# A norm factor kept in PSUM, and a weight split's ramp in PSUM, in a replanned attention and MoE kernel

## The chip, the cores and the metric

The kernel runs on one core of a Trainium2 chip. The metric is the device time of one execution in microseconds; the time of a kernel is the median of its runs.

## The reference

Three steps follow one another, all in float32. Clustered attention on 2 batch elements, 8 heads, 768 positions and a head dimension of 64; its output, 1536 tokens of 512 numbers, goes through a normed gated block and then through a second block.

```python
q_assign = np.argmax(einsum(q_n, c_n)); k_assign = np.argmax(einsum(k_n, c_n))    # 16 clusters per head
scores = np.where(q_assign == k_assign, scale * q @ k.T, -1e9)
attn = softmax(scores);  x = attn @ v                      # per head; heads side by side give x: 1536 x 512
rms = np.sqrt(np.mean(x * x, axis=-1, keepdims=True) + 1e-06)
xn = x / rms * rms_g
g = xn @ w_gate;  h = g * (1.0 / (1.0 + np.exp(-g))) * (xn @ w_val)     # 512 -> 1536
x = h @ w_out                                                            # 1536 -> 512
r = np.maximum(x @ w_in, 0.0);  out = (s * (r * r) + b) @ w_out2         # 512 -> 2048 -> 512
```

## The kernel before

Heads are numbered 0 to 15: 0 to 7 are batch element 0, 8 to 15 batch element 1. For each head the kernel finds the clusters (`assign_*`), the maximum of each row of scores (`rowmax` on TensorE, `rowmax_out` at L424 on VectorE), the scores and their exponentials (L447, L448, L453), splits the exponentials into a half-precision high part (`cast`, on GpSimd at L458 or on ScalarE at L460) and a rest (`rest`, GpSimd, L464), multiplies with the values (L477, L487) and divides (`pv_out`, L498 to L500). The table `pc` in `P` names, per head, the chunks whose cast GpSimd does.

When the eight heads of a batch element are done, `rms_scale` works out one factor per token: it adds the partial sums of squares (L530), scales (L531), and calls `rsqrt` (L506 to L511), which is a shift, a subtraction from a constant and three Newton steps of three operations each, all on VectorE and on tiles of 128x6 in SBUF, named rx, rr and rw. `rms_norm` (L539) multiplies the tokens by it; transposes (L546), `rms_x` (L553, L555) make the operands xh and xl of the next block.

The weights come as 64-bit words that `split_w` turns into float32 and then into a high and a low part. ScalarE makes two ramps of the exponent byte, `a` (L606) and `b` (L607); VectorE joins them to the exponent (L610, from b and a, both in SBUF, into a) and puts the mantissa in (L611, from raw and a, both in SBUF, into a); ScalarE copies the high part (L614), GpSimd subtracts (L617). `wtmp` holds one pair a, b, so that splits follow one another. `plan_weights` plans the splits of four slices of the hidden dimension, f = 0 to 3, three matrices each (j = 0, 1, 2: gate, value, out).

The first two pairs of slices are filler for TensorE inside the attention of heads 8 to 15: `m_mm` (L623), `m_tanh` (L925), `m_gate` (L929), `m_val` (L933), `m_hi` (L937), `m_lo` (L941), `m_pr` (L656). They write PSUM tiles of the tag "g", of which there are two (`b_g=2`). The banks of these two are the second buffer of the row maxima of heads 0 to 7; `switch` closes that pool and opens "g", once the row maxima of head 7 are done (`gsw`).

All of the attention and of this filler is an order written out by a planner (`Plan`): every step is added with its engine, a cost in us, what it reads and writes, the buffers that it takes and a priority; the planner starts the step that can begin first, and among those that can begin within `look` of it the one of least priority value. The leads in `P` (`lt`, `lh`, ... `lr`, `lg`, `lk`, `rg`) set the priorities. Each engine then works through its steps in the planned order, and a step waits only for its inputs and its buffers. What follows the planned part (`run_items`: the other pairs of the first block, and the second block) has a fixed order.

Of the kernel before, what the change touches and what calls it, by code (L numbers as in the profile page):

```python
# [20 lines left out]
F32 = mybir.dt.float32  # L21
# [9 lines left out]
BIG = 2.0 ** 100  # L31

P = dict(
    nat=(1, 1, 1, 1, 1, 1, 1, 1, 1, 1, 1, 1, 1, 1, 1, 1), pc=((0, 1, 2, 3, 4), (3,), (0, 4), (0, 4), (0, 1, 3, 4),
    (4,), (1, 2, 3, 4), (1,), (1, 3, 4), (0, 4), (0, 1, 3), (0,), (0, 1, 2, 3), (2, 3, 4), (0, 1, 2, 3), (0, 1)),
    b_wp=2, b_raw=2, b_hp=4, b_tp=2, b_wt=1, b_q4=3, b_a32=5, b_a16=6, b_vsp=2, b_up=2, pvb=2, b_pm=1, b_g=2,
    b_pv=1, b_s=3, look=(0.2, 0.14, 0.14, 0.0, 1.07), fifo=2.5, ni=1, nx=5, lg=462.36, rg=-6.19, lk=147.75, nd=2,
    l1=53.02, l2=-28.36, li=347.3, ho=(0.0, 0.0, 0.0, 0.0, 0.0, 0.0, 0.0, 0.0, 0.0, 0.0, 0.0, 0.0, 0.0, 0.0, 0.0,
    0.0), lt=(-36.0, -253.71), lh=(-125.63, 332.03), ld=(93.0, -61.97), la=(-0.63, 344.08), le=(563.62, -285.56),
    lm=(118.57, 144.43), lo=(307.47, -175.69), ll=(-131.36, -42.83), lx=(24.87, 357.66), ls=(-128.3, 6.07),  # L40
    lc=(-68.33, 7.5), lv=(-27.58, -184.46), lw=(-142.18, -496.74), ly=(64.26, 270.33), lq=(35.78, -22.17),
    lp=(-408.39, -161.62), lz=(-203.89, -3.37), lr=(11.8, -52.43)
)

class Plan:
# [100 lines left out]
def attention_moe_moe2_kernel(  # L146
# [357 lines left out]
    def rsqrt(y, x, w):  # L504

        nc.vector.tensor_scalar(w.bitcast(I32), x.bitcast(I32), 1, None, op0=ALU.logical_shift_right)  # L506
        nc.vector.tensor_scalar(y.bitcast(I32), w.bitcast(I32), -1.0, float(0x5F3759DF), op0=ALU.mult, op1=ALU.add)
        for _ in range(3):
            tt(out=w, in0=y, in1=y, op=ALU.mult)
            stt(out=w, in0=w, scalar=-0.5, in1=x, op0=ALU.mult, op1=ALU.mult)  # L510
            stt(out=y, in0=w, scalar=1.5, in1=y, op0=ALU.add, op1=ALU.mult)  # L511

    def rms_sq(b, c, h0, h1, j):
# [12 lines left out]
    jk2 = {}  # L526

    def rms_scale(b):
        x, r, w = (sm.tile([128, NCH], F32, tag=f"{n}{b}", name=n) for n in ("rx", "rr", "rw"))
        tt(out=x, in0=ss[b][:, :, 0], in1=ss[b][:, :, 1], op=ALU.add)  # L530
        nc.vector.tensor_scalar(x, x, 1.0 / DM, 1e-6, op0=ALU.mult, op1=ALU.add)  # L531
        rsqrt(r, x, w)
        r_t[b] = r
        for t in range(b * S // TB, (b + 1) * S // TB):
            xh[t], xl[t] = new_x(t)
# [61 lines left out]
        dma(out=raw.rearrange("p (k n) -> p k n", n=n)[:, :, 0:n - 3], in_=src)  # L597
        return raw

    def split_w(raw, to, j):  # L600


        top = raw.rearrange("p (n e) -> p n e", e=8)[:, :, 4]
        low = raw.bitcast(I32).rearrange("p (n e) -> p n e", e=2)[:, :, 0]
        a, b = (wtmp.tile([128, 512], F32, tag=n, name=n) for n in ("wa", "wb"))
        act(out=a, in_=top, func=ACTF.Relu, scale=2.0 ** 27, bias=ebias)  # L606
        act(out=b, in_=top, func=ACTF.Relu, scale=-2.0 ** 27, bias=ebias)  # L607
        yield
# [186 lines left out]
    def last_head():  # L795
        early.close()
        xpool[2] = xpool[3] = pool(ctx, "x1p", side="right")

    for i in range(NH):
        b, h = heads(i)  # L800
        p = i // 2
# [249 lines left out]
```

## Time and profile before

| | us |
|---|---|
| median of 3 runs | 829.93 |
| lowest, highest run | 826.66, 831.51 |
| the profiled execution | 827.66 |
| its span, first to last instruction | 825.70 |
| TensorE busy in the span | 780.9 (95%) |
| VectorE, ScalarE, GpSimd busy | 519.4, 469.1, 444.4 |
| mean granted TensorE clock | 0.994 |

The planned part lasts until about 300 us, the fixed order from there to the end. The rows call TensorE PE (PEld: its weight loads), VectorE DVE, ScalarE ACT, GpSimd POOL and SyncE SP. An instruction's row gives its start from the span's begin, its duration, its line and the tiles that it writes and reads; in brackets how long the engine was idle before it and what ended that. An instruction that is held up after it was issued shows as a longer duration, not as idle time.

### The profile page before, as it was taken

To read this page: it belongs to the slowest core of one execution; us is meant where nothing else is said; L and a number is where in the kernel's file an instruction comes from. 1 tells how busy PE (TensorE), PEld (TensorE's weight loads), DVE (VectorE), ACT (ScalarE), POOL (GpSimd) and SP (SyncE) were. 2 spreads that over 40 slices of the span, in tenths; PEclk is the share of its full clock that TensorE was granted. 3 is DMA by queue.
4 is the path that set the end of the run, shared out by engine and by line. 5 is a ranking of instruction groups with operands and counts; after the bars stand their busy time and mean duration, and the time that the engine had idled before them with its cause. 6 is when DMAs were issued, how large, how long until landed. Compare 5 with 4: busy or idle time off the path is not lost.

```text
span 825.7 us, 14199 instructions
## 1 busy us (share of the span) xinstructions
PE 780.9 (95%) x5505; PEld 722.5 (88%) x5505; DVE 519.4 (63%) x845; ACT 469.1 (57%) x883; POOL 444.4 (54%) x400
## 2 busy tenths in 40 slices
PE   3899898699999799999999999999999999999998
PEld 1688776589998689999999999998999998989897
DVE  6789898898876676554645446554465555555533
ACT  5486778556858555442434435555566566665532
POOL 7599999677999534332323226455343343343421
PEclk9999999799999999999999999999999999999999
DMA  7498766155430223311311212220121121220012
GB/s 114 86 138 146 159 135 122 30 106 134 98 87 27 78 77 102 101 55 50 102 51 56 72 52 78 82 93 30 32 97 52 52 77 52 78 74 29 1 39 114
DMA packets 98818, 65.13 MB, mean 79 GB/s; under 512 B 64992, under 2 KB 89664, under 8 KB 98752
## 3 DMA queue, kind: packets, MB, share of 16 engines
q1 hardware_dynamic: 98752, 64.24, 31.3%
q8 instruction: 43, 0.70, 0.4%
q14 instruction: 23, 0.19, 0.1%
HBM read 48.45 MB, written 3.15 MB: 62 GB/s over the span
## 4 chain that ended last, share of the span: by engine, by line
PE 81%; DVE 10%; POOL 3%; issue 2%; DMA 2%; ACT 2%; SPq 0%; DVEq 0%; POOLq 0%
PE pg L623 28%; PE po L658 16%; PE po L656 10%; PE pl L623 10%; PE pv L487 4%; PE mps L416 4%; PE sps L447 3%; PE sps L448 3%; PE pv L477 2%; DVE mt L424 2%; PE pg L656 1%; DVE wa L610 1%; DVE vs L355 1%; DVE wa L611 1%; DMA q<-ot 1%
## 5 line engine op out<-in xcount | busy, mean ns | idle before, releaser
L646 POOL TENSOR_TENSOR gl<-hv,gh 128x384 fp32r<-128x384 f32 x104 | 107.2, 1030 | 214.0 <-ACT gh L645 195.2
L623 PE MATMUL pg<-xh,wh 128*128 128x384 f32 x480 | 162.1, 338 | 1.5 <-ACT wh L614 1.1
L623 PE MATMUL pg<-xh,wl 128*128 128x384 f32 x480 | 161.4, 336 | 0.7 <-POOL wl L617 0.7
L623 PE MATMUL pg<-xl,wh 128*128 128x384 f32 x480 | 161.2, 336 | 0.0
L617 POOL TENSOR_TENSOR wl<-wa,wh 128x512 fp32r<-128x512 f32 x74 | 95.9, 1296 | 115.8 <-ACT wh L614 110.1
L464 POOL TENSOR_TENSOR al<-a,ah 128x768 f16<-128x768 f32 x80 | 137.2, 1729 | 14.8 <-ACT ah L460 13.5
L610 DVE SCALAR_TENSOR_TENSOR wa<-wb,wa 128x512 int32<-128x512 f32 x74 | 54.2, 732 | 97.4 <-ACT wa L606 97.1
L666 DVE TENSOR_TENSOR acc<-po,acc 128x512 f32<-128x512 f32 (+1 forms) x160 | 95.1, 620 | 29.6 <-PE po L658 19.2
L453 ACT ACTIVATE a<-sps 128x384 f32<-128x384 f32 x192 | 86.7, 490 | 44.6 <-PE sps L448 42.8
L606 ACT ACTIVATE wa<-raw,ebias 128x512 f32<-128x512 int8 x74 | 56.2, 759 | 77.2 <-POOL wl L617 77.1
L424 DVE TENSOR_REDUCE mt<-mps 128x1 fp32r<-128x768 f32 x96 | 90.3, 944 | 13.9 <-PE mps L416 13.8
L623 PEld LDWEIGHTS pg<-xh,wh 128*128 128x128 f32 x480 | 90.1, 188 | 4.0 <-ACT wh L614 1.4
L623 PEld LDWEIGHTS pg<-xl,wh 128*128 128x128 f32 x480 | 90.1, 188 | 1.2
L623 PEld LDWEIGHTS pg<-xh,wl 128*128 128x128 f32 x480 | 90.0, 188 | 1.1 <-POOL wl L617 1.1
L643 DVE SCALAR_TENSOR_TENSOR th<-pg,th 128x384 f32<-128x384 f32 x64 | 35.5, 554 | 71.2 <-ACT th L642 71.0
L658 PE MATMUL po<-wh,gl 128*128 128x512 f32 x192 | 75.1, 391 | 0.6 <-POOL gl L646 0.6
L658 PE MATMUL po<-wl,gh 128*128 128x512 f32 x192 | 75.0, 391 | 0.0
L607 ACT ACTIVATE wb<-raw,ebias 128x512 f32<-128x512 int8 x74 | 56.6, 765 | 32.1 <-DVE wa L610 23.7
L658 PE MATMUL po<-wh,gh 128*128 128x512 f32 x192 | 74.7, 389 | 0.0
L447 PE MATMUL sps<-q 128*128 128x384 f32 x192 | 71.8, 374 | 2.9 <-ACT a L453 1.7
L614 ACT ACTIVATE wh<-wa 128x512 fp32r<-128x512 f32 x74 | 46.7, 631 | 48.3 <-PE pg L623 22.7
L611 DVE SCALAR_TENSOR_TENSOR wa<-raw,wa 128x512 int32<-128x512 int32 x74 | 72.4, 978 | 1.7
(134 smaller groups left out, 1746.5 us busy)
## 6 DMA issues: line engine op xcount, KB each, us to landing
raw<-in_moe_w_out_dram SPq DMA_DIRECT2D x30, 511.6 KB, 3.5
raw<-in_moe_w_in_dram SPq DMA_DIRECT2D x16, 510.5 KB
raw<-in_moe_w_gate_dram SPq DMA_DIRECT2D x14, 510.5 KB, 3.4
raw<-in_moe_w_val_dram SPq DMA_DIRECT2D x14, 510.5 KB, 3.4
q<-q SPq DMA_DIRECT2D x14, 384.0 KB, 4.6
q<-q SPq DMA_DIRECT2D x28, 192.0 KB, 4.1
vr<-in_v_dram SPq DMA_DIRECT2D x8, 384.0 KB
out_dram<-acc SPq DMA_DIRECT2D x12, 256.0 KB, 2.0
```

The lines of the kernel that those rows point to most:

```text
L424: nc.vector.tensor_reduce(out=mt_of[i][:, c:c + 1], in_=m_t.pop((i, c))[:, :, 0:HALF], axis=AX.XY, op=ALU.max)
L447: nc.tensor.matmul(ps[:, 0:HALF], lhsT=x[:, 2, ks], rhs=x[:, 1, cs], start=True, stop=False)
L453: act(out=a_t[i, c][:, e * HALF:(e + 1) * HALF], in_=s_t.pop((i, c, e))[:, 0:HALF], func=ACTF.Exp, scale=scale)
L464: nc.gpsimd.tensor_tensor(out=al, in0=a_t.pop((i, c)), in1=ah_t[i, c], op=ALU.subtract)
L610: stt(out=ai, in0=b, scalar=2.0 ** 31, in1=a, op0=ALU.min, op1=ALU.subtract, reverse1=True)
L611: stt(out=ai, in0=low, scalar=5, in1=ai, op0=ALU.logical_shift_right, op1=ALU.bitwise_or)
L617: nc.gpsimd.tensor_tensor(out=l, in0=a, in1=h.bitcast(F32), op=ALU.subtract)
L623: nc.tensor.matmul(ps, lhsT=a[:, kk * 128:kk * 128 + 128], rhs=x[:, kk, :], start=(kk == m == 0), stop=(kk == KC - 1 and m == 2),)
L646: nc.gpsimd.tensor_tensor(out=gl, in0=hv, in1=gh.bitcast(F32), op=ALU.subtract)
L656: nc.tensor.matmul(ps, lhsT=a[:, cs], rhs=x, start=st[0], stop=st[1])
L658: nc.tensor.matmul(ps, lhsT=x[:, cs], rhs=a, start=st[0], stop=st[1])
L666: tt(out=ac, in0=ps, in1=ac, op=ALU.add)
```

## The change

`rms_scale` puts x and w into one PSUM tile and leaves r in SBUF; the tile is of tag "g" for batch element 0 (which therefore waits for `gsw`) and of tag "s", that of the scores, for batch element 1. The Newton step is written so that each of its operations has one operand in PSUM and one in SBUF; the number of operations is the same, and `rsqrt` is used in its new form by the centroids too. `split_w` can be given a tile for its ramp a: for f = 0 and 1 (six splits) that is a PSUM tile of tag "g", written by L606's operation, read and written by L610's, read by L611's; the first wait of these six loads is now for `gsw` too. `switch` is planned earlier in the list, beside the end of head 7. The planner's cost for the VectorE part of these splits is 1.5 in place of 2.45 us. `pc` and nearly all leads are new, which gives another order; the count of casts on GpSimd goes from 20 to 17 for heads 0 to 7 and from 22 to 21 for heads 8 to 15.

```diff
-    nat=(1, 1, 1, 1, 1, 1, 1, 1, 1, 1, 1, 1, 1, 1, 1, 1), pc=((0, 1, 2, 3, 4), (3,), (0, 4), (0, 4), (0, 1, 3, 4),
-    (4,), (1, 2, 3, 4), (1,), (1, 3, 4), (0, 4), (0, 1, 3), (0,), (0, 1, 2, 3), (2, 3, 4), (0, 1, 2, 3), (0, 1)),
+    nat=(1, 1, 1, 1, 1, 1, 1, 1, 1, 1, 1, 1, 1, 1, 1, 1), pc=((1, 2, 3, 4), (4,), (2,), (1, 4), (0, 4), (0, 1, 3),
+    (4,), (0, 1, 2), (1, 2, 3), (0, 4), (2, 3), (0, 2, 4), (3, 4), (0, 1, 3, 4), (0, 1, 4), (0, 2)), b_wp=2,
...
-    b_pv=1, b_s=3, look=(0.2, 0.14, 0.14, 0.0, 1.07), fifo=2.5, ni=1, nx=5, lg=462.36, rg=-6.19, lk=147.75, nd=2,
+    look=(0.12, 0.1, 0.11, 0.0, 0.79), fifo=2.5, ni=1, nx=5, lg=400.05, rg=-24.19, lk=74.25, nd=2, l1=149.68,
...
-            tt(out=w, in0=y, in1=y, op=ALU.mult)
-            stt(out=w, in0=w, scalar=-0.5, in1=x, op0=ALU.mult, op1=ALU.mult)
+            tt(out=w, in0=x, in1=y, op=ALU.mult)
+            stt(out=w, in0=w, scalar=-0.5, in1=y, op0=ALU.mult, op1=ALU.mult)
...
     def rms_scale(b):
-        x, r, w = (sm.tile([128, NCH], F32, tag=f"{n}{b}", name=n) for n in ("rx", "rr", "rw"))
+        ps = ps_s.tile([128, 512], F32, tag="s", name="rps") if b else ps_g[-1].tile([128, 512], F32, tag="g", name="rpg")
+        x, w = ps[:, 0:NCH], ps[:, 16:16 + NCH]
+        r = sm.tile([128, NCH], F32, tag=f"rr{b}", name="rr")
...
-    def split_w(raw, to, j):
+    def split_w(raw, to, j, ramp=None):
...
-        act(out=a, in_=top, func=ACTF.Relu, scale=2.0 ** 27, bias=ebias)
+        ai = a.bitcast(I32)
+        up_ = ramp() if ramp else a
+        ui = up_.bitcast(I32)
+        act(out=up_, in_=top, func=ACTF.Relu, scale=2.0 ** 27, bias=ebias)
         act(out=b, in_=top, func=ACTF.Relu, scale=-2.0 ** 27, bias=ebias)
         yield
-        ai = a.bitcast(I32)
-        stt(out=ai, in0=b, scalar=2.0 ** 31, in1=a, op0=ALU.min, op1=ALU.subtract, reverse1=True)
-        stt(out=ai, in0=low, scalar=5, in1=ai, op0=ALU.logical_shift_right, op1=ALU.bitwise_or)
+        stt(out=ui, in0=b, scalar=2.0 ** 31, in1=up_, op0=ALU.min, op1=ALU.subtract, reverse1=True)
+        stt(out=ai, in0=low, scalar=5, in1=ui, op0=ALU.logical_shift_right, op1=ALU.bitwise_or)
...
         if h == H - 1:
-            add("DVE", 2.4, call(rms_scale, b), r=[("ss", b, c, x) for c in range(NCH) for x in (H - 3, H - 1)],
-                w=[("r", b)], prio=at("lr"))
+            g = "s" if b else "g"
+            if b == 0:
+                add("SP", 0.0, switch, r=[("maxed", H - 1, c) for c in range(NCH)], w=[("gsw", 0)], prio=-1e5)
+            add("DVE", 2.4, call(rms_scale, b), r=[*([] if b else [("gsw", 0)]), *(("ss", b, c, x) for c in range(NCH) for x in (H - 3, H - 1))],
+                w=[("r", b), (g, ("n", b))], new=[(g, ("n", b))], prio=at("lr"))
...
-            st["g"] = split_w(load_w(1, f % NF[1], j), wp[0], j)
+            st["g"] = split_w(load_w(1, f % NF[1], j), wp[0], j, ramp if f < 2 else None)
...
+        def ramp():
+            return ps_g[-1].tile([128, 512], F32, tag="g", name="wg")
+
         wn = 3 * f + j
+        g = [("g", ("w", f, j))] if f < 2 else []
+        if g:
+            r = [*r, ("gsw", 0)]
...
-        add("DVE", 2.45, nx, r=[("raw", (f, j))], w=[("wt", (f, j))], prio=prio)
+        add("DVE", 1.5 if g else 2.45, nx, r=[("raw", (f, j)), *g], w=[("wt", (f, j))], prio=prio)
```

## Rows read from the trace of the kernel before

**Rows 1.** Busy time by stretch: start:end, length, busy and count per engine, clock, DMA.

```profile
60.00:148.00 88.00, 79.19 (x963) 66.32 (x960) 77.50 (x121) 68.06 (x146) 82.56 (x68) 1.00 0.70 136
148.00:156.00 8.00, 2.73 (x14) 1.81 (x12) 7.59 (x14) 3.24 (x7) 6.78 (x8) 0.80 0.23 49
156.00:164.00 8.00, 7.08 (x57) 6.64 (x57) 5.70 (x8) 3.43 (x6) 2.91 (x2) 0.56 0.01 2
164.00:183.00 19.00, 17.42 (x205) 15.53 (x203) 18.18 (x24) 10.05 (x22) 13.01 (x9) 1.00 0.50 89
183.00:262.00 79.00, 78.94 (x825) 74.37 (x826) 63.95 (x95) 57.30 (x126) 71.94 (x64) 1.00 0.40 97
262.00:300.00 38.00, 31.41 (x271) 27.77 (x271) 25.33 (x49) 23.88 (x43) 19.95 (x15) 1.00 0.18 56
300.00:826.00 526.00, 521.40 (x2814) 497.13 (x2813) 274.20 (x448) 268.76 (x468) 202.57 (x181) 1.00 0.21 66
```

**Rows 2.** Timeline of VectorE, 147 to 157 us: start, duration, operation.

```profile
147.83 0.49 DVE L530 TENSOR_TENSOR rx<-ss 128x6 f32<-128x6 f32 x1
...
149.14 1.57 DVE L506 TENSOR_SCALAR rw<-rx 128x6 int32<-128x6 int32 x1
...
150.75 1.57 DVE L507 TENSOR_SCALAR rr<-rw 128x6 int32<-128x6 int32 x1
...
153.31 1.49 DVE L511 SCALAR_TENSOR_TENSOR rr<-rw,rr 128x6 f32<-128x6 f32 x1
...
155.83 0.17 DVE L511 SCALAR_TENSOR_TENSOR rr<-rw,rr 128x6 f32<-128x6 f32 x1
```

**Rows 3.** Timeline of GpSimd, 148 to 162 us.

```profile
149.04 3.25 POOL L464 TENSOR_TENSOR al<-a,ah 128x768 f16<-128x768 f32 x2
...
153.14 1.64 POOL L464 TENSOR_TENSOR al<-a,ah 128x768 f16<-128x768 f32 x1
...
160.86 1.65 POOL L464 TENSOR_TENSOR al<-a,ah 128x768 f16<-128x768 f32 x1 [6.09 <-ACT ah L460]
```

**Rows 4.** Waits of TensorE, 140 to 185 us: total, times, longest.

```profile
PE mps L416 <- DVE mt L424: 5.9, 2, 5.7
```

**Rows 5.** Timeline of VectorE, 280 to 284 us, the second batch element's factor.

```profile
280.92 0.17 DVE L506 TENSOR_SCALAR rw<-rx 128x6 int32<-128x6 int32 x1
...
282.93 0.17 DVE L511 SCALAR_TENSOR_TENSOR rr<-rw,rr 128x6 f32<-128x6 f32 x1
```

**Rows 6.** Line 498 in the whole span: least, middle and longest time (ns).

```profile
L498 DVE TENSOR_SCALAR dn<-pv,vsc x16: 183/224/227, 48.4 to 276.1; 128x6 f32<-128x6 f32 x16
```

**Rows 7.** Groups of VectorE, 80 to 183 us: busy us, mean ns, idle before.

```profile
L611 DVE SCALAR_TENSOR_TENSOR wa<-raw,wa 128x512 int32<-128x512 int32 x4 | 6.6, 1656 | 0.1
...
L610 DVE SCALAR_TENSOR_TENSOR wa<-wb,wa 128x512 int32<-128x512 f32 x4 | 4.5, 1127 | 0.0
```

**Rows 8.** Lines 610 and 611 in the whole span: least, middle, longest (ns).

```profile
L610 DVE SCALAR_TENSOR_TENSOR wa<-wb,wa x74: 648/693/2129, 88.4 to 766.3; 128x512 int32<-128x512 f32 x74
L611 DVE SCALAR_TENSOR_TENSOR wa<-raw,wa x74: 674/693/2215, 90.5 to 767.0; 128x512 int32<-128x512 int32 x74
```

**Rows 9.** Groups of GpSimd, 80 to 140 us.

```profile
L464 POOL TENSOR_TENSOR al<-a,ah 128x768 f16<-128x768 f32 x21 | 36.2, 1737 | 2.6 <-ACT ah L460 2.2
...
L458 POOL CAST ah<-a 128x768 f16<-128x768 f32 x10 | 9.6, 970 | 0.4 <-ACT a L453 0.4
```

**Rows 10.** SyncE's issue of head 7's row maxima, from the timeline.

```profile
114.21 0.73 SPq L437 DMA_DIRECT2D q<-mT  x1
```

**Rows 11.** Timelines of ScalarE, TensorE and VectorE around the first filler tile.

```profile
141.25 0.77 ACT L606 ACTIVATE wa<-raw,ebias 128x512 f32<-128x512 int8 x1
...
168.25 0.35 PE L623 MATMUL pg<-xh,wh 128*128 128x384 f32 x1
...
175.66 0.54 DVE L929 SCALAR_TENSOR_TENSOR th<-th,pg 128x384 f32<-128x384 f32 x1
...
177.70 2.21 DVE L611 SCALAR_TENSOR_TENSOR wa<-raw,wa 128x512 int32<-128x512 int32 x1
```

More of the change, by code (lines that the diff above doesn't have):

```diff
@@ L33 @@
 P = dict(
-    nat=(1, 1, 1, 1, 1, 1, 1, 1, 1, 1, 1, 1, 1, 1, 1, 1), pc=((0, 1, 2, 3, 4), (3,), (0, 4), (0, 4), (0, 1, 3, 4),
-    (4,), (1, 2, 3, 4), (1,), (1, 3, 4), (0, 4), (0, 1, 3), (0,), (0, 1, 2, 3), (2, 3, 4), (0, 1, 2, 3), (0, 1)),
-    b_wp=2, b_raw=2, b_hp=4, b_tp=2, b_wt=1, b_q4=3, b_a32=5, b_a16=6, b_vsp=2, b_up=2, pvb=2, b_pm=1, b_g=2,
-    b_pv=1, b_s=3, look=(0.2, 0.14, 0.14, 0.0, 1.07), fifo=2.5, ni=1, nx=5, lg=462.36, rg=-6.19, lk=147.75, nd=2,
[L38 to L42, printed above, removed]
+    nat=(1, 1, 1, 1, 1, 1, 1, 1, 1, 1, 1, 1, 1, 1, 1, 1), pc=((1, 2, 3, 4), (4,), (2,), (1, 4), (0, 4), (0, 1, 3),
+    (4,), (0, 1, 2), (1, 2, 3), (0, 4), (2, 3), (0, 2, 4), (3, 4), (0, 1, 3, 4), (0, 1, 4), (0, 2)), b_wp=2,
+    b_raw=2, b_hp=4, b_tp=2, b_wt=1, b_q4=3, b_a32=5, b_a16=6, b_vsp=2, b_up=2, pvb=2, b_pm=1, b_g=2, b_pv=1, b_s=3,
+    look=(0.12, 0.1, 0.11, 0.0, 0.79), fifo=2.5, ni=1, nx=5, lg=400.05, rg=-24.19, lk=74.25, nd=2, l1=149.68,
+    l2=-350.1, li=338.5, ho=(0.0, 0.0, 0.0, 0.0, 0.0, 0.0, 0.0, 0.0, 0.0, 0.0, 0.0, 0.0, 0.0, 0.0, 0.0, 0.0),
+    lt=(-189.93, -2.05), lh=(-448.38, 422.36), ld=(-3.9, 149.46), la=(-88.91, 803.76), le=(565.06, -56.15),
+    lm=(203.83, 159.64), lo=(303.34, -350.19), ll=(-114.17, 202.72), lx=(213.92, 136.69), ls=(-278.65, -61.07),
+    lc=(-230.27, 190.06), lv=(-145.62, -192.3), lw=(-314.4, -353.37), ly=(90.09, 340.84), lq=(163.99, -175.9),
+    lp=(-539.47, -378.15), lz=(-271.35, 74.48), lr=(15.1, -221.59)
 )
@@ L797, in last_head, with switch @@
         xpool[2] = xpool[3] = pool(ctx, "x1p", side="right")
+    def switch():
+        att_m.close()
+        ps_g.append(pool(att_m, "ps_g0", P["b_g"], space=PSUM))
     for i in range(NH):
@@ L899, in ld_ @@
         def ld_():
-            st["g"] = split_w(load_w(1, f % NF[1], j), wp[0], j)
+            st["g"] = split_w(load_w(1, f % NF[1], j), wp[0], j, ramp if f < 2 else None)
         def nx():
             wts[f, j] = next(st["g"])
+        def ramp():
+            return ps_g[-1].tile([128, 512], F32, tag="g", name="wg")
         wn = 3 * f + j
+        g = [("g", ("w", f, j))] if f < 2 else []
+        if g:
+            r = [*r, ("gsw", 0)]
         r = [*r, *([("wseq", wn - 1)] if wn else [])]
         add("SP", .52, ld_, r=r, w=[("raw", (f, j)), ("wseq", wn)], new=[("raw", (f, j))], prio=prio, lat=1.7)
-        add("ACT", 1.53, nx, r=[("raw", (f, j)), *([("wtq", wn - 1)] if wn else [])], w=[("wtq", wn), ("wt", (f, j))], new=[("wt", (f, j))], prio=prio)
-        add("DVE", 2.45, nx, r=[("raw", (f, j))], w=[("wt", (f, j))], prio=prio)
+        add("ACT", 1.53, nx, r=[("raw", (f, j)), *([("wtq", wn - 1)] if wn else [])], w=[("wtq", wn), ("wt", (f, j)), *g], new=[("wt", (f, j)), *g], prio=prio)
+        add("DVE", 1.5 if g else 2.45, nx, r=[("raw", (f, j)), *g], w=[("wt", (f, j))], prio=prio)
         add("ACT", .63, nx, r=[("wt", (f, j))], w=[(f"wt{j}", f, "h")], new=[(f"wt{j}", f)], prio=prio)
@@ L951, in m_acc @@
         project_add(pg_t.pop((n, t, "p", c)), t, c, TB, n == 0)
-    def switch():
-        att_m.close()
-        ps_g.append(pool(att_m, "ps_g0", P["b_g"], space=PSUM))
     def m_xh(t, c):
@@ L965, in m_xl @@
         )
-    add("SP", 0.0, switch, r=[("maxed", H - 1, c) for c in range(NCH)], w=[("gsw", 0)], prio=-1e5)
     def gx(t, part):
```

## The prediction

> **What bounds the kernel now.** Read the busy time by stretch first, with the two numbers beside each other: TensorE's busy time and the length. From 300 us on TensorE is busy 521.4 of 526 us, and from 183 to 262 us 78.9 of 79 us [rows 1]. There TensorE is the limit, and the change neither removes nor adds a matmul. What can be won lies in the gaps before: 8.8 us idle from 60 to 148 us, 5.3 us from 148 to 156, 0.9 us from 156 to 164 with a granted clock of 0.56, 1.6 us from 164 to 183, 6.6 us from 262 to 300 [rows 1]. That is 23 us, without the first 60 us and the last few.
>
> Second, who holds TensorE up in these gaps. From 140 to 185 us one wait of 5.7 us stands out, for VectorE's row maximum [rows 4]. VectorE's timeline says why the maximum is late: from 147.83 to 156.00 us it works through the thirteen operations of `rms_scale`. They have 6 elements per partition each, and yet two take 1.57 us and one 1.49, while the last takes 0.17 [rows 2]. GpSimd's timeline beside it gives the cause: its two subtractions run from 149.04 to 152.29, 1.63 us each; the shift that starts at 149.14 ends at 150.71, and the next operation that starts at 150.75 ends at 152.32. The operation from 153.31 ends at 154.80, GpSimd's from 153.14 at 154.78 [rows 2, 3]. These VectorE operations end with GpSimd's, whatever their own size. For batch element 1 the same code meets an idle GpSimd, and its twelve operations after L530 go by in 0.2 us each [rows 5].
>
> [...]
>
> Third, the weight splits. L610 takes 0.648 us and L611 0.674 us at least, 2.13 and 2.2 at most [rows 8]. The four splits that VectorE does between 80 and 183 us cost 1.127 + 1.656 = 2.78 us each, and VectorE never sat idle before them [rows 7]: it is then the late engine, along with GpSimd (82.6 busy of 88 us from 60 to 148) [rows 1].
>
> **The change part by part.**
>
> *The factor of batch element 0.* All thirteen operations stay. Twelve of them now have a PSUM operand; L530 still reads two SBUF tiles and keeps its 0.49 us [rows 2]. Unhindered, twelve at 0.2 us are 2.4 us [rows 5]. No row shows VectorE writing PSUM. The nearest is a 128x6 operation that reads PSUM, 0.224 us against 0.17 [rows 5, 6], so 0.05 us more; I take that for eleven operations, 0.5 us, with 0 and twice that (a read and a write) as ends, since nothing excludes either. New length 0.5 + 2.4 + 0.5 = 3.4 us against 8.2: **4.8 us less** (4.3 to 5.3). It lies on the path: TensorE's 5.7 us wait ends with it [rows 4].
>
> [...]
>
> *The clock behind it.* [...] From 60 to 148 us it is idle a tenth of the time in short pieces and the clock is 1.00 [rows 1]. Without the long gap I expect 1.00. TensorE's 7.1 us would be 7.1 x 0.56 = 4.0 us, but VectorE has 5.7 us of work in these 8 [rows 1], so at most 2.3 us return. I take **2.0 us** (0 to 2.3).
>
> *The ramps.* Six splits have L610 and L611 with one SBUF operand each. At the middle durations, 0.69 + 0.69 us [rows 8], a split costs 1.4 us in place of 2.8. The four before 183 us would give 5.6 us, 1.4 each. From 60 to 148 us, where three lie, GpSimd is late as well, with 5.4 us idle in 88 [rows 1]; of 4.2 us I take half, **2.1 us** (0 to 4.2). The fourth lies between 164 and 183 us, where VectorE has 18.2 of 19 us and GpSimd 13.0 [rows 1]: **1.4 us** (0 to 1.4). The two after it fall under TensorE's full stretch and give nothing. ScalarE's write of the ramp into PSUM has no row; ScalarE is busy 68 of 88 us [rows 1], so I set it at nothing; if that cover were gone it would be a tenth or two of 0.77 us [rows 11] six times, under 1 us.
>
> *The casts.* GpSimd gives up three casts of 0.97 us [rows 9] for heads 0 to 7 and one after, and ScalarE, with room, takes them. Of 2.9 us I take **0.5** (0 to 2.9), since VectorE is late there too.
>
> *The wait for head 7.* The six loads and the first factor now come after the row maxima of head 7, done at about 114 us [rows 10]. The factor starts at 148 us anyway. Of the splits, two ran before 114 us; they move behind it. The first filler matmul, which needs two splits and the normed tokens, is at 168.25 us [rows 11], 54 us later. At a split in 20 us it is still met; ramps wait in ScalarE's queue, and SyncE's loads stand behind `gsw` with the q and k loads of later heads queued after them, which the planned order puts where the wait is over. I cost it at nothing; late filler leaves TensorE what it has now between 164 and 183 us, 1.6 us [rows 1].
>
> *The new order.* Nothing in the trace of before shows it. Its bounds are the gaps that the present order leaves in a stretch of this kind: 6.6 us, from 262 to 300 us [rows 1], could come once more or go. For batch element 1 the factor shares the scores' three buffers, after the last scores, and costs 0.5 us more by the same PSUM price. I take 2 us lost for order and that together.
>
> Sum: 4.8 + 2.0 + 2.1 + 1.4 + 0.5 - 2 = 8.8, rounded to **8 us** because GpSimd may follow close behind. What is late next is GpSimd from 60 to 148 us, and TensorE itself from some 175 us on. The profiled execution had 827.66 us (span 825.70), 2.3 below the median of the runs, 829.93; it would become 819.7, and the median **822 us**.
>
> **The rivals.**
>
> *GpSimd takes VectorE's place, and the gain is eaten.* For it: GpSimd at 82.6 of 88 us [rows 1]. Then ramps, casts and clock give nothing, 4.8 us stay from the factor, and the new order takes 2 to 5: 827 to 830, no measurable change. Against it: GpSimd itself was idle 6.1 us at 155 to 161 us, waiting for a chain that VectorE held [rows 3]. That PSUM operands don't free VectorE from GpSimd is the other way to this result: 830, the order aside.
>
> *The ramps hold the filler's buffers, and it is slower.* There are two "g" tiles. A filler tile holds one from its first matmul at 168.25 until VectorE's operation ends at 176.2, 8 us for 12 matmuls, about 2.1 us of TensorE's work. A ramp holds one from ScalarE's start to the end of L611: the fourth split from 141.25 to 179.9, 38.7 us [rows 11]. Ramps that hold a buffer for 28 us in all push 28 / 8 x 2.1 = 7.3 us of filler out of the attention into a time with no cover: 822 + 7 = 829. At 55 us it is 14.4 us, and the time 836. It decides from about 45 us, where 12 us go (834). For it: the 38.7 us. Against it: the first three ramps come before any filler, and the planner counts the buffer.
>
> **How the numbers follow.** Two runs of this kernel differ enough that 0.5%, 4 us, is about what can be told from no change: faster is below 825.8, slower above 834.1. My forecast of a gain (814 to 825.8) has 0.61. The first rival has 0.23. The third case, the ramps or a worse order of that size, has 0.16. The lower end is the sum with the upper bounds of all terms, 5.3 + 2.3 + 4.2 + 1.4 + 2.9 = 16, and no loss, 814; I go to 813. The upper end reaches into the slow case, to 834.
>
> **What would show it.** Right: the twelve operations at about 0.2 us although GpSimd is busy, VectorE's stretch for the factor under 4 us, no wait of TensorE over 2 us there, a granted clock of 1.00 after it, six splits at 0.7 + 0.7 us. Wrong: ramps that live tens of us while filler tiles are wanted; TensorE idle between 160 and 260 us of the new trace; a longer gap than 6.6 us at the end of the attention. What I can't see at all is the new order, and a gap of over 8 us anywhere in it would make the forecast wrong though every price holds.

## The result and the profile after

| | us |
|---|---|
| median after (817.16 to 821.7) | 818.12 |
| median before, same chip (826.66 to 831.51) | 828.9 |
| ratio of after to before, 95% interval | 0.9867 [0.9838, 0.9896] |
| the profiled execution after, its span | 817.16, 815.2 |
| mean granted TensorE clock | 0.996 |

The changed kernel is 10.8 us faster by the medians. The two spans differ by 825.7 - 815.2 = 10.5 us.

First the busy time by stretch of the kernel after, with the columns of [rows 1]. The cuts are put where the same work stands: the second stretch holds the factor, the third ends behind the first filler tile's start.

```profile
60.00:141.80 81.80, 78.69 (x955) 66.64 (x955) 70.46 (x119) 68.16 (x148) 75.86 (x65) 1.00 0.74 141
141.80:150.00 8.20, 6.83 (x58) 5.46 (x58) 7.75 (x21) 5.18 (x11) 8.20 (x9) 0.79 0.33 72
150.00:158.00 8.00, 7.96 (x69) 7.17 (x68) 7.89 (x10) 6.04 (x13) 8.00 (x5) 1.00 0.02 5
158.00:180.00 22.00, 19.62 (x231) 17.64 (x230) 19.67 (x35) 14.37 (x30) 15.51 (x14) 1.00 0.65 129
180.00:260.00 80.00, 79.87 (x838) 74.63 (x837) 58.51 (x86) 57.73 (x123) 72.29 (x63) 1.00 0.36 96
260.00:298.00 38.00, 31.14 (x229) 29.82 (x227) 23.58 (x48) 19.74 (x39) 12.93 (x11) 0.96 0.13 43
298.00:816.00 518.00, 512.96 (x2765) 488.53 (x2763) 268.91 (x440) 265.36 (x463) 200.24 (x180) 1.00 0.20 65
```

Up to the factor TensorE now idles 81.80 - 78.69 = 3.1 us, where it idled 8.8 us from 60 to 148 us before [rows 1]. In the stretch that holds the factor it is busy 6.83 of 8.2 us; before it was 2.73 of 8. The gap at the end of the attention is as it was, 6.9 us against 6.6 [rows 1].

The timeline of VectorE after, through the factor of batch element 0 (start, duration, operation), answers to [rows 2]:

```profile
141.73 0.46 DVE L532 TENSOR_TENSOR rpg<-ss 128x6 f32<-128x6 f32 x1
142.23 0.17 DVE L533 TENSOR_SCALAR rpg<-rpg 128x6 f32<-128x6 f32 x1
...
144.47 0.16 DVE L511 SCALAR_TENSOR_TENSOR rr<-rpg,rr 128x6 f32<-128x6 f32 x1
```

And GpSimd's timeline beside it, which answers to [rows 3]:

```profile
142.88 3.26 POOL L464 TENSOR_TENSOR al<-a,ah 128x768 f16<-128x768 f32 x2
```

GpSimd's two subtractions run from 142.88 to 146.14, and VectorE's small operations go by under them at 0.17 us each. The factor lasts from 141.73 to 144.63, 2.9 us, where it lasted from 147.83 to 156.00 [rows 2].

TensorE's waits after, 135 to 185 us (total, times, longest), answer to [rows 4]; the 5.7 us wait is gone, and these are the two largest:

```profile
PE asps L363 <- DVE dn L498: 2.0, 1, 2.0
PE sps L447 <- DVE ot L398: 0.8, 1, 0.8
```

The ramps, after, in the whole span (least, middle, longest in ns, first and last start), answer to [rows 8]; a tile named wg is the ramp in PSUM, wa the one in SBUF. The last two lines are ScalarE's operation that makes the ramp.

```profile
L614 DVE SCALAR_TENSOR_TENSOR wg<-wb,wg x6: 682/689/697, 121.3 to 196.7; 128x512 int32<-128x512 f32 x6
...
L615 DVE SCALAR_TENSOR_TENSOR wa<-raw,wa x68: 676/693/2035, 208.5 to 756.6; 128x512 int32<-128x512 int32 x68
L615 DVE SCALAR_TENSOR_TENSOR wa<-raw,wg x6: 686/687/689, 122.0 to 197.5; 128x512 int32<-128x512 int32 x6
...
L611 ACT ACTIVATE wa<-raw,ebias x68: 747/755/768, 206.3 to 755.1; 128x512 f32<-128x512 int8 x68
...
L611 ACT ACTIVATE wg<-raw,ebias x6: 709/723/748, 118.8 to 195.2; 128x512 f32<-128x512 int8 x6
```

The six splits cost VectorE 0.69 + 0.69 us with no outlier, where four cost 2.78 each [rows 7].

Where the 10.5 us come from is read best from four marks, taken alike in the profiled execution of every kernel below: start of the factor's first operation, end of its last, first filler matmul, start of the attention's last matmul with the values (L477).

| kernel | factor starts | ends | first filler | last values matmul | span |
|---|---|---|---|---|---|
| before | 147.8 | 156.0 | 168.3 | 275.8 | 825.7 |
| after | 141.7 | 144.6 | 155.8 | 266.1 | 815.2 |
| a_full | 141.8 | 144.7 | 155.9 | 267.8 | 818.3 |
| a_rms0_ramp1 | 143.0 | 150.4 | 163.2 | 275.9 | 824.6 |
| a_rms1_ramp0 | 145.1 | 148.9 | 160.7 | 274.0 | 822.7 |
| a_rms0_ramp0 | 145.1 | 152.3 | 165.0 | 277.9 | 828.9 |
| b_rms1 | 150.7 | 153.7 | 164.8 | 272.3 | 822.3 |
| b_ramp | 146.8 | 154.9 | 166.3 | 281.8 | 831.7 |
| b_rms1_ramp | 146.6 | 149.5 | 160.8 | 275.8 | 825.8 |
| acode_oldP | 150.9 | 154.9 | 188.3 | 277.5 | 841.7 |
| c_ramp1pl | 141.9 | 144.8 | 156.0 | 277.7 | 824.5 |
| c_ramp4 | 142.5 | 145.4 | 156.6 | 281.1 | 825.0 |
| d_same_ramp1 | 142.1 | 145.0 | 156.2 | 270.7 | 819.2 |
| d_same_ramp4 | 141.8 | 144.7 | 155.9 | 267.1 | 814.6 |

From before to after, 6.1 us are won ahead of the factor, 5.3 in it, and about 1 us is lost again behind it.

### The profile page after: what moved, and what is told of

The parts are those of the page before. It is cut to its first block, busy times and chain, and to the rows that moved or that the text cites. A ratio compares the mean times of both kernels' runs of the same rounds, so it can differ in the third digit from the quotient of the medians.

```text
span 815.2 us, 14207 instructions
## 1 busy us (share of the span) xinstructions
PE 780.0 (96%) x5505; PEld 722.4 (89%) x5505; DVE 505.5 (62%) x845; ACT 470.8 (58%) x887; POOL 437.1 (54%) x396
## 4 chain that ended last, share of the span: by engine, by line
PE 84%; DVE 6%; POOL 4%; ACT 2%; issue 2%; DMA 0%; POOLq 0%; DVEq 0%; ACTq 0%
PE pg L627 29%; PE po L662 16%; PE po L660 10%; PE pl L627 10%; PE mps L416 4%; PE pv L487 4%; PE sps L447 3%; PE sps L448 3%; PE pv L477 2%; DVE mt L424 2%; PE pg L660 2%; POOL al L464 1%; DVE w L379 1%; POOL wl L621 1%; PE tr L548 1%
## 5 line engine op out<-in xcount | busy, mean ns | idle before, releaser
L464 POOL TENSOR_TENSOR al<-a,ah 128x768 f16<-128x768 f32 x80 | 135.4, 1710 | 15.9 <-ACT ah L460 15.1
L614 DVE SCALAR_TENSOR_TENSOR wa<-wb,wa 128x512 int32<-128x512 f32 x68 | 49.2, 724 | 103.6 <-ACT wa L611 98.0
L424 DVE TENSOR_REDUCE mt<-mps 128x1 fp32r<-128x768 f32 x96 | 90.2, 946 | 13.2 <-PE mps L416 12.2
L611 ACT ACTIVATE wa<-raw,ebias 128x512 f32<-128x512 int8 x68 | 51.4, 756 | 72.3 <-POOL wl L621 72.3
L649 ACT ACTIVATE gh<-hv 128x384 fp32r<-128x384 f32 x104 | 54.1, 520 | 30.0 <-DVE hv L644 28.5
```

Source lines behind the costliest of these rows:

```text
L424: nc.vector.tensor_reduce(out=mt_of[i][:, c:c + 1], in_=m_t.pop((i, c))[:, :, 0:HALF], axis=AX.XY, op=ALU.max)
L464: nc.gpsimd.tensor_tensor(out=al, in0=a_t.pop((i, c)), in1=ah_t[i, c], op=ALU.subtract)
L649: act(out=gh, in_=hv, func=ACTF.Copy)
```

## The experiments

All kernels compute the whole reference; nothing is left out. Times are medians, ratios go to runs of the kernel before on the same chip. A ratio is not the quotient of the two medians shown; the two differ by up to 0.24%, 2 us, so a difference below is given by both where it matters. The first letter tells the base: a is the kernel after, b the kernel before; c and d are the kernel after with other numbers of ramps.

### The order, the factor and the ramps, in the new order

Four kernels share the planned order of after. a_full is after itself. In the others the factor's x and w, or the ramps, or both, go back to SBUF, without a new plan.

Of a_rms0_ramp1 and a_rms0_ramp0:

```diff
-        ps = ps_s.tile([128, 512], F32, tag="s", name="rps") if b else ps_g[-1].tile([128, 512], F32, tag="g", name="rpg")
-        x, w = ps[:, 0:NCH], ps[:, 16:16 + NCH]
...
+        x, r, w = (sm.tile([128, NCH], F32, tag=f"{n}{b}", name=n) for n in ("rx", "rr", "rw"))
```

Of a_rms1_ramp0 and a_rms0_ramp0:

```diff
-            st["g"] = split_w(load_w(1, f % NF[1], j), wp[0], j, ramp if f < 2 else None)
+            st["g"] = split_w(load_w(1, f % NF[1], j), wp[0], j)
```

a_full:

> The changed kernel once more, beside the three below on one chip. Both theories: 818 us as measured (817.2 to 821.7), ratio to before 0.987.

a_rms0_ramp1, the factor back in SBUF:

> The changed kernel, its order untouched, with the factor's x and w back in SBUF; the ramps stay in PSUM. Theory of the forecast (operands in PSUM free VectorE from GpSimd, and that lies on the path): operations of the factor that start while GpSimd runs end with it again, 1.5 us at most, the factor takes 6 to 8 us in place of 2.9, TensorE waits 3 to 5 us longer for the row maximum, and the granted clock falls behind it: 4 to 7 us slower than the changed kernel, 822 to 825. Rival (the order carries the gain, GpSimd is the late engine): under 1.5 us slower, 818 to 820.

a_rms1_ramp0, the ramps back in SBUF:

> The changed kernel, its order untouched, with the six ramps back in SBUF; the factor stays in PSUM. Theory of the forecast: L614 and L615 take 0.9 to 2 us in place of 0.69 where GpSimd is busy, 1 to 1.4 us more for each split, of which four lie before TensorE is full: 2 to 5 us slower, 820 to 823. Rival (GpSimd late, or the splits lie where TensorE is full in the new order): under 1 us, 818 to 819.

a_rms0_ramp0, the new order alone:

> The changed kernel's order alone: factor and ramps both back in SBUF. Theory of the forecast: the two losses add up, 6 to 11 us slower than the changed kernel, 824 to 829, so the order by itself gives nothing or little. Rival (the order carries the gain): 818 to 821. If the losses do not add up, the engine that was hidden behind the one is the bound of the other.

| kernel | median us | ratio to before (829.76 us) |
|---|---|---|
| a_full | 819.19 | 0.9865 [0.9817, 0.9912] |
| a_rms0_ramp1 | 824.69 | 0.9943 [0.9913, 0.9972] |
| a_rms1_ramp0 | 826.28 | 0.9946 [0.992, 0.9973] |
| a_rms0_ramp0 | 831.42 | 0.9996 [0.9968, 1.0025] |

The new order alone moves nothing that can be measured. On top of it the factor brings 0.9996 - 0.9946 = 0.50%, 4.2 us, the ramps 0.9996 - 0.9943 = 0.53%, 4.4 us, and both 1.31%, 10.9 us. By the medians it is 5.1, 6.7 and 12.2 us. That both bring 2.3 us more than the two apart by the ratios is within the intervals, and by the medians the two add up, so it is not shown. The factor's loss, 5.5 us from a_full to a_rms0_ramp1, fell into the expected 4 to 7; the ramps' loss, 7.1 us, was expected at 2 to 5, and that of both, 12.2 us, at 6 to 11.

What the factor in SBUF does is seen in a_rms0_ramp1: VectorE's timeline, then GpSimd's, then TensorE's wait of 135 to 190 us.

```profile
143.13 1.57 DVE L531 TENSOR_SCALAR rx<-rx 128x6 f32<-128x6 f32 x1
144.74 1.56 DVE L506 TENSOR_SCALAR rw<-rx 128x6 int32<-128x6 int32 x1
...
147.20 1.58 DVE L509 TENSOR_TENSOR rw<-rx,rr 128x6 f32<-128x6 f32 x1
148.81 0.17 DVE L510 SCALAR_TENSOR_TENSOR rw<-rw,rr 128x6 f32<-128x6 f32 x1
```

```profile
143.03 3.24 POOL L464 TENSOR_TENSOR al<-a,ah 128x768 f16<-128x768 f32 x2
...
147.12 1.64 POOL L464 TENSOR_TENSOR al<-a,ah 128x768 f16<-128x768 f32 x1
```

```profile
PE sps L447 <- DVE ot L398: 6.3, 1, 6.3
```

It is the picture of [rows 2, 3] once more, in another order: 1.6 us for 6 elements until GpSimd's last subtraction ends at 148.76, and 0.17 from there on. TensorE pays 6.3 us for the operation that is queued behind the factor on VectorE; in the kernel after the same wait is 0.8 us. Only the place of x and w differs between the two.

What the ramps in SBUF do is seen in a_rms1_ramp0, whose factor is in PSUM: VectorE's timeline, then TensorE's busy time by stretch, then its waits from 180 to 220 us.

```profile
121.57 0.68 DVE L614 SCALAR_TENSOR_TENSOR wa<-wb,wa 128x512 int32<-128x512 f32 x1
122.29 1.20 DVE L615 SCALAR_TENSOR_TENSOR wa<-raw,wa 128x512 int32<-128x512 int32 x1
133.22 1.88 DVE L614 SCALAR_TENSOR_TENSOR wa<-wb,wa 128x512 int32<-128x512 f32 x1 [0.46 <-ACT wb L612]
135.13 2.18 DVE L615 SCALAR_TENSOR_TENSOR wa<-raw,wa 128x512 int32<-128x512 int32 x1
145.09 1.33 DVE L532 TENSOR_TENSOR rpg<-ss 128x6 f32<-128x6 f32 x1
...
185.86 1.39 DVE L615 SCALAR_TENSOR_TENSOR wa<-raw,wa 128x512 int32<-128x512 int32 x1
191.65 1.38 DVE L615 SCALAR_TENSOR_TENSOR wa<-raw,wa 128x512 int32<-128x512 int32 x1
```

```profile
180.00:220.00 40.00, 38.02 (x375) 35.40 (x375) 33.88 (x46) 28.41 (x58) 34.55 (x29) 1.00 0.40 108
```

```profile
PE mps L416 <- DVE mt L424: 2.0, 2, 1.1
```

Two slow splits put the factor 3.4 us later (145.1 against 141.7), and two more, at 186 and 192 us, keep TensorE waiting for row maxima for 2.0 us in a stretch where it was full in the kernel after, 40.00 of 40 us. L532, the one operation of the factor that still reads two SBUF tiles, took 1.33 us here.

### The parts in the order of before

b_rms1 puts the factor alone into PSUM, with the new form of the Newton step. b_ramp gives a PSUM tile of tag "g" to the ramps of the splits that follow `switch` in the old order, (f, j) = (0, 2), (1, 0), (1, 1) and (1, 2), without telling the planner. b_rms1_ramp does both. In acode_oldP the code is that of after, with the ramps planned, and `P` is that of before.

The edit of b_rms1 to the kernel before; the new lines are those of after:

```diff
-            tt(out=w, in0=y, in1=y, op=ALU.mult)
-            stt(out=w, in0=w, scalar=-0.5, in1=x, op0=ALU.mult, op1=ALU.mult)
+            tt(out=w, in0=x, in1=y, op=ALU.mult)
+            stt(out=w, in0=w, scalar=-0.5, in1=y, op0=ALU.mult, op1=ALU.mult)
...
-        x, r, w = (sm.tile([128, NCH], F32, tag=f"{n}{b}", name=n) for n in ("rx", "rr", "rw"))
+        ps = ps_s.tile([128, 512], F32, tag="s", name="rps") if b else ps_g[-1].tile([128, 512], F32, tag="g", name="rpg")
...
```

Of b_ramp and b_rms1_ramp, beside after's `split_w`:

```diff
-            st["g"] = split_w(load_w(1, f % NF[1], j), wp[0], j)
+            st["g"] = split_w(load_w(1, f % NF[1], j), wp[0], j, (lambda: ps_g[-1].tile([128, 512], F32, tag="g", name="wg")) if (f, j) in ((0, 2), (1, 0), (1, 1), (1, 2)) else None)
```

Of acode_oldP to the kernel after, one line of `P` for all:

```diff
-    look=(0.12, 0.1, 0.11, 0.0, 0.79), fifo=2.5, ni=1, nx=5, lg=400.05, rg=-24.19, lk=74.25, nd=2, l1=149.68,
+    b_pv=1, b_s=3, look=(0.2, 0.14, 0.14, 0.0, 1.07), fifo=2.5, ni=1, nx=5, lg=462.36, rg=-6.19, lk=147.75, nd=2,
...
```

b_rms1:

> The kernel before, its order untouched, with the factor's x and w in PSUM alone (and the Newton step in its new form). Theory of the forecast: the factor takes 2.9 us in place of 8.2, TensorE's wait of 5.7 us shrinks to under 1 and the granted clock does not fall behind it: 5 to 7 us faster, ratio 0.992 to 0.994. Rival (GpSimd takes VectorE's place): 0 to 3 us faster.

b_ramp:

> The kernel before, its order untouched, with the ramps of the four splits that come after the switch in PSUM tiles of tag g; the plan does not know of it. The fourth split's ramp is written by ScalarE at 141 us and read by VectorE at 177 to 180. Forecast's third case (a ramp holds a filler's buffer): the second filler tile waits for the ramp, TensorE waits 5 us or more between 165 and 185 us, 2 to 8 us slower than before. Theory of the ramps' gain alone: VectorE saves 1.5 us in the third and fourth split, 1 to 3 us faster.

b_rms1_ramp:

> Both of the above in the order of before. Forecast: the factor's 5 to 7 us gain plus whatever the run with the ramps alone shows; if the plan's buffer count matters, it is slower than the run with the factor alone.

acode_oldP:

> The changed code with the old table of leads and casts: the planner makes a new order from the old leads, knowing of the PSUM tiles, of the wait for head 7 and of the lower cost. Theory of the forecast: 4 to 8 us faster than before, 821 to 825, since the prices hold in any order. Rival (the new leads carry the gain): within 2 us of before or slower.

| kernel | median us | ratio to before (830.13 us) |
|---|---|---|
| b_rms1 | 823.45 | 0.9902 [0.9872, 0.9932] |
| b_ramp | 839.37 | 1.0093 [1.0063, 1.0122] |
| b_rms1_ramp | 830.77 | 1.0004 [0.9976, 1.0031] |
| acode_oldP | 842.62 | 1.0141 [1.0114, 1.0169] |

The factor is worth 0.98% in the old order with nothing else changed, 8.1 us, or 6.7 by the medians; 5 to 7 were expected. VectorE's timeline in b_rms1, and GpSimd's subtractions over it:

```profile
150.69 0.53 DVE L532 TENSOR_TENSOR rpg<-ss 128x6 f32<-128x6 f32 x1
...
153.50 0.17 DVE L511 SCALAR_TENSOR_TENSOR rr<-rpg,rr 128x6 f32<-128x6 f32 x1
```

```profile
151.93 3.25 POOL L464 TENSOR_TENSOR al<-a,ah 128x768 f16<-128x768 f32 x2
```

The ramps cost 0.9% there (b_ramp), and 1.0% on top of the factor: they eat its gain. b_ramp shows how, in ScalarE's and VectorE's timelines, then TensorE's waits from 135 to 190 us and its busy time.

```profile
139.84 0.74 ACT L609 ACTIVATE wg<-raw,ebias 128x512 f32<-128x512 int8 x1
...
175.71 0.69 DVE L613 SCALAR_TENSOR_TENSOR wa<-raw,wg 128x512 int32<-128x512 int32 x1
```

```profile
PE mps L416 <- DVE mt L424: 5.9, 2, 5.7
PE pg L625 <- DVE th L931: 3.4, 1, 3.4
```

```profile
160.00:180.00 20.00, 15.97 (x159) 14.70 (x159) 15.72 (x21) 7.97 (x17) 9.95 (x7) 0.84 0.44 77
```

The ramp of (1, 0) is written at 139.8 and read until 176.4: it stands for 36.6 us in one of the filler's two tiles. The filler has one tile left; TensorE waits 3.4 us until VectorE has read it, is busy 16 of 20 us, and the granted clock is 0.84; the kernel before has 18.6 of 20 us and 0.92 there. In b_rms1_ramp the same ramp stands 31 us, with the same wait of 3.4 us. In both the ramp of (1, 1) stands 10.4 us, and TensorE waits for a filler tile again, 1.8 us. The 5.7 us wait of [rows 4] is still there in b_ramp, as the factor is in SBUF. b_ramp was expected 2 to 8 us slower, with a wait of 5 us or more; by the medians it is 9.2 us slower.

acode_oldP tells the planner of the ramps and is worse still, where 4 to 8 us of gain were expected if the prices hold in any order; in the order of the old leads they do not come to a gain. ScalarE's, VectorE's and TensorE's timelines:

```profile
148.30 0.73 ACT L611 ACTIVATE wg<-raw,ebias 128x512 f32<-128x512 int8 x1
...
185.60 0.69 DVE L615 SCALAR_TENSOR_TENSOR wa<-raw,wg 128x512 int32<-128x512 int32 x1
...
188.26 0.33 PE L627 MATMUL pg<-xh,wh 128*128 128x384 f32 x1
```

The same ramp stands for 38 us, planned so, and the first filler matmul comes at 188.3 us, 20 us later than before [rows 11]. Whether the ramp keeps that filler back, or the plan had it late for another reason, no run tells. A reservation in the plan alone does not keep ramps short; in the kernel after, under the new leads, the longest is 12.7 us, from 156.9 to 169.7, and the others take 2.9 to 6.4. So the table of leads and casts, worth nothing by itself, decides whether the changed code pays: 0.9865 against 1.0141 with the same code. Which of its entries does it was not tried.

### How many ramps, with a new plan and without

c_ramp1pl has ramps in PSUM for f = 0 only, c_ramp4 for f = 0 to 3; in both the planner knows and makes a new order with after's leads. d_same_ramp1 and d_same_ramp4 make the same two choices in the planned order of after as it is.

Of c_ramp4; d_same_ramp4 has the first pair of lines only, and c_ramp1pl and d_same_ramp1 have 1 in place of 4:

```diff
-            st["g"] = split_w(load_w(1, f % NF[1], j), wp[0], j, ramp if f < 2 else None)
+            st["g"] = split_w(load_w(1, f % NF[1], j), wp[0], j, ramp if f < 4 else None)
...
-        g = [("g", ("w", f, j))] if f < 2 else []
+        g = [("g", ("w", f, j))] if f < 4 else []
```

c_ramp1pl:

> The kernel after with ramps in PSUM for slice f = 0 only (three splits in place of six), the planner told so and the order planned anew with the same leads. If the gain of the ramps lies in the first three splits, which stand before the first filler tile, this gives 817 to 821 us, ratio 0.985 to 0.990. If each ramp in PSUM is worth as much as every other, half of the 6.7 us is lost: 822 to 824. If the fit of leads and plan is what counts, any change of the plan under old leads loses some: 824 to 832.

c_ramp4:

> The kernel after with ramps in PSUM for all twelve planned splits (f = 0 to 3), the planner told so and the order planned anew with the same leads. If planned reservations make ramps harmless, it is 815 to 820 us, ratio 0.982 to 0.990, with nothing to be won since the last six splits lie under a full TensorE. If ramps take the filler's two tiles even when planned, the filler loses buffers in 183 to 260 us and it is 825 to 840, ratio 0.995 to 1.012, with TensorE under 78 of 80 us busy there.

d_same_ramp1:

> The kernel after in its own planned order, ramps in PSUM for slice f = 0 only (three splits); the three of f = 1 are back in SBUF, their reservation in the plan stays. If the three splits ahead of the first filler and of its second tile carry the gain and the loss of the run with a new plan was its order, this gives 818 to 821.5 us, ratio 0.985 to 0.990. If the ramps of f = 1 are worth something of their own, as TensorE's 2 us idle from 180 to 220 us without them suggests, it is 821.5 to 826, ratio 0.990 to 0.995, with TensorE at about 38 of 40 us busy there.

d_same_ramp4:

> The kernel after in its own planned order, ramps in PSUM for all twelve planned splits; the six of f = 2 and 3 are not reserved in the plan and take a filler tile when their turn comes. If the loss of the run with a new plan was its order alone, this gives 815 to 820 us, ratio 0.982 to 0.989. If a ramp that the plan does not know costs about 0.26 us per us that it stands, and each stands 3 to 6 us as in the new plan, it is 822 to 827. If one of them stands 20 us or more, as unplanned ramps did in the order of before, it is above 827, with TensorE waiting for VectorE's th at a filler tile.

| kernel | ramps | order | median us | ratio to before |
|---|---|---|---|---|
| c_ramp1pl | 3 | new | 826.59 | 0.9952 [0.9934, 0.9971] |
| d_same_ramp1 | 3 | after's | 823.93 | 0.9922 [0.989, 0.9953] |
| a_full | 6 | after's | 819.19 | 0.9865 [0.9817, 0.9912] |
| d_same_ramp4 | 12 | after's | 817.09 | 0.9854 [0.9807, 0.9901] |
| c_ramp4 | 12 | new | 826.4 | 0.9935 [0.9912, 0.9958] |

What was expected came out as the third case of c_ramp1pl, the second of d_same_ramp1 and the first of d_same_ramp4; c_ramp4 fell into its second range, but its waits are not for filler tiles. The same twelve ramps give 0.9854 in one order and 0.9935 in the other. The six additional ramps of d_same_ramp4 stand only 2.9 to 3.5 us each, though the planner does not know of them. TensorE waits 0.4 + 0.3 us for tiles that they hold; they cost nothing that the median shows, and win nothing that can be told from after either. In c_ramp4 the front half is as in after, with the first filler at 156.6 us. From 180 to 260 us TensorE is busy 78.15 of 80 us, 1.7 us less than in after. Most of the loss is at the end of the attention, where TensorE's longest wait from 260 to 300 us, and its busy time there, are

```profile
PE tr L548 <- DVE xn L541: 8.6, 4, 6.4
```

```profile
260.00:300.00 40.00, 30.01 (x280) 27.40 (x279) 21.84 (x44) 16.61 (x31) 14.59 (x11) 0.79 0.04 15
```

In the kernel after this wait is 0.3 us in all in that stretch, TensorE is busy 33.14 of the 40 us, and the granted clock is 0.96. So leads that fit one plan need not fit its neighbour: what c_ramp4 measures is its order first, and the ramps second. For c_ramp1pl that is not shown: its interval overlaps that of d_same_ramp1.

d_same_ramp1 tells what the ramps of f = 1 are worth: 0.9922 - 0.9865 = 0.57%, 4.7 us, with intervals that overlap; to d_same_ramp4, on the same chip, it is 6.8 us by the medians, so the ramps from f = 1 on are worth something. Its trace shows where part of that lies, again in TensorE's busy time:

```profile
180.00:220.00 40.00, 38.03 (x345) 35.57 (x344) 34.23 (x48) 28.18 (x59) 34.54 (x29) 1.00 0.40 106
```

## Why the prediction was right, and where it was off

The forecast, 822 us and a gain of 8, came out at 818 and a gain of 10.8, inside the range. Term by term:

**The factor, right.** 4.8 us were taken, with 5.3 as the upper end; it became 5.3 us shorter. That an operation with one operand in PSUM goes by unhindered beside GpSimd, on which this term and that of the ramps rest, was the author's assumption; before shows at most L498, which reads PSUM and never took more than 0.227 us [rows 6]. After shows it: 0.16 to 0.17 us under GpSimd's subtractions, and 0.682 to 0.697 us for the ramps' two operations, the second pair of them (132.21 to 133.69) beside a subtraction that starts at 131.95. With x and w in SBUF L509 took 1.58 us in a_rms0_ramp1. Its worth in time was 8.1 us in the old order and 4.2 in the new one without the ramps (6.7 and 5.1 by the medians). In the old order that is 1.5 to 2.9 us more than the 5.2 us by which it became shorter (150.7 to 153.7). The clock behind it is 1.00 from 140 to 180 us in b_rms1, against 0.56 from 156 to 164 us [rows 1], but b_rms1 was at 0.91 from 100 to 140 us, before the factor; whether the clock is the rest stays open.

**The PSUM price, seven times too high.** The forecast put 0.05 us on each operation, from the row of an operation on another line [rows 5, 6]. The rows to compare are these, L510 of after and then of before, in ns:

```profile
L510 DVE SCALAR_TENSOR_TENSOR rpg<-rpg,rr x3: 171/173/173, 143.0 to 144.3; 128x6 f32<-128x6 f32 x3
```

```profile
L510 DVE SCALAR_TENSOR_TENSOR rw<-rw,rx x6: 165/166/166, 153.1 to 282.7; 128x6 f32<-128x6 f32 x6
```

One read and one write of PSUM cost 7 ns here. What makes L498 [rows 6] longer, no run tells. ScalarE's write of the ramp, set at nothing with a tenth or two of 0.77 us as the far end, became shorter: 0.723 us against 0.755.

**The ramps, right in kind, mis-sized.** 3.5 us were forecast; they measured 4.4 us without the factor in PSUM and 6.7 with it, by the medians 6.7 and 7.1. The steps that failed are two. "The two after it fall under TensorE's full stretch and give nothing" took the full stretch of before [rows 1] for that of the new order; there TensorE idles 2.0 of 40 us without these ramps (a_rms1_ramp0, d_same_ramp1). And "of 4.2 us I take half", because GpSimd was late as well, was too careful: in the new order two splits lie ahead of the factor, not three, and they cost VectorE 3.2 us more in SBUF (L615 1.20 and 2.18, L614 2.6 together, against 2.8 for all four), and all of it arrived, the factor coming 3.4 us later. GpSimd, idle 81.8 - 75.9 = 5.9 us up to the factor as against 5.4 of 88 before [rows 1], did not take VectorE's place, and the sum's rounding from 8.8 down to 8 on its account went the wrong way.

**The order, 2 us lost: within what was measured.** The order alone gave 0.9996 [0.9968, 1.0025], 2.7 us gained to 2.1 us lost; by the medians it loses 1.7 us. It brings the factor 2.7 us forward (145.1 against 147.8) and gives that back by the attention's end (277.9 against 275.8). The casts cannot be told from it: they are part of a_rms0_ramp0.

**The clock, half right.** "A granted clock of 1.00 after it" was wrong for the 5 us behind the factor, and right from 150 us on:

```profile
141.80:145.00 3.20, 2.25 (x11) 1.28 (x10) 2.79 (x15) 2.81 (x8) 3.20 (x4) 1.00 0.82 179
145.00:150.00 5.00, 4.57 (x47) 4.19 (x48) 4.97 (x8) 2.36 (x4) 5.00 (x6) 0.66 0.01 3
```

The 2.0 us set TensorE's 0.56 from 156 to 164 us against its 1.00 from 60 to 148 us [rows 1], and took the gap between for the cause. No run tells what lowers the clock: a_full was as idle from 144 to 146 us, busy 0.95 of 2 us, and was at 1.00 until 160 us. Over the span the mean went from 0.994 to 0.996; by estimate, the span times what the clock lacks of 1, that is 5.0 and 3.3 us, 1.7 us less, where 2.0 were taken. But a_full, the same kernel, had a mean of 0.993, 5.7 us, so two executions differ by more than this term, and its size is not shown.

**No wait of TensorE over 2 us there, a gap of 6.6 us at the end:** right, with 2.0 us as the longest and 6.9 us.

**The rivals.** That GpSimd eats the gain is refuted by the factor's 0.17 us operations under its subtractions and by a_rms0_ramp1 and a_rms1_ramp0. That the ramps hold the filler's buffers is a real mechanism, at the place given (3.4 us of wait in b_ramp), but its price does not go by the length of the hold. The prediction had 7.3 us for 28 us of hold in all, and 14.4 for 55. The four ramps of b_rms1_ramp stand 55.0 us in all, and it lost 1.02% to b_rms1, 8.5 us, or 7.3 by the medians. The six of the kernel after stand 32.5 us in all, and TensorE waits for no filler tile from 135 to 185 us; the twelve of d_same_ramp4 stand 52.6 us and cost nothing that the median shows. What the prediction had against this rival, that the planner counts the buffer, was no good reason: in acode_oldP it counts it and lets a ramp stand 38 us. The traces suggest a better one: whether TensorE's next step wants a tile while the ramp stands. In b_ramp the second filler tile comes right behind the first and waits; in the kernel after TensorE works on the attention from 159 to 165 us, under the 12.7 us ramp, and starts the second tile at 165.6. No run moves that alone, so it is not shown.

## What to carry to other kernels

When small VectorE operations end exactly with the GpSimd operation beside them, put one operand of each into PSUM: here 1.6 us became 0.17, for 7 ns. A tile borrowed from another stage's buffers costs, as far as these traces tell, when that stage wants one while it stands, so look at what comes next on the stage's engine, and put writer and reader side by side in the order, before borrowing; borrowing for six splits was worth 0.5% to 0.8% in one order, and for four of them, unplanned, it cost 0.9% to 1.0% in another. And leads fitted to one plan can say little about a plan with other steps: compare a change in a fixed order first.

## What was not expected of the hardware

The granted clock falls at places that differ between executions of the same kernel. In the profiled execution shown first the kernel after had TensorE busy 0.90 of 2 us from 144 to 146 us; its clock fell right behind that and was at 0.50 from 148 to 150 us:

```profile
144.00:146.00 2.00, 0.90 (x4) 0.30 (x2) 1.90 (x7) 1.97 (x5) 2.00 (x2) 1.00 0.05 8
146.00:148.00 2.00, 1.96 (x30) 1.99 (x30) 1.97 (x5) 1.36 (x3) 2.00 (x5) 0.64 0.04 8
148.00:150.00 2.00, 2.00 (x20) 1.90 (x18) 2.00 (x2) 0.00 (x0) 2.00 (x2) 0.50 0.00 0
```

a_full, the same kernel, was busy 0.95 of 2 us there, and its clock stayed up until 160 us and fell later:

```profile
144.00:146.00 2.00, 0.95 (x4) 0.31 (x3) 1.90 (x7) 1.97 (x4) 2.00 (x2) 1.00 0.15 28
...
140.00:160.00 20.00, 16.49 (x169) 13.51 (x168) 19.44 (x34) 15.53 (x32) 20.00 (x18) 1.00 0.30 65
160.00:180.00 20.00, 18.44 (x215) 16.73 (x216) 16.35 (x31) 11.11 (x23) 11.98 (x9) 0.91 0.62 122
260.00:300.00 40.00, 33.19 (x254) 31.77 (x253) 24.29 (x49) 21.80 (x42) 14.81 (x13) 0.91 0.18 55
```

Its span was 818.3 us against 815.2. By the same estimate as above, 0.09 of 20 and of 40 us are 1.8 + 3.6 = 5.4 us in a_full; in the execution shown first 0.21 of 8.2 (141.8 to 150) and 0.04 of 38 us (260 to 298) are 1.7 + 1.5 = 3.2 us. The difference, 2.2 us, is a good part of the 3.1 us between the spans.

Beside GpSimd's subtractions L509 took 1.58 us in a_rms0_ramp1, with both operands in SBUF, and 0.17 us in the kernel after, in the same order. So the runs show beyond [rows 2] that an operation of the factor with one operand in PSUM is not held.
